# Seven quarter products for the second matmul too, in the last two token tiles

## The chip, the cores and the metric

The kernel runs on one core of one Trainium2 chip, in one launch. The metric is the device time of one execution in microseconds, the median of several runs. Lower is better.

## The reference

Linear attention per head, an RMS norm over the head's 64 outputs, and a feed-forward block over all tokens:

```python
kv = np.einsum('bhsd,bhse->bhde', k, v)                # 8 batches, 8 heads, 576 tokens, 64 wide
out = np.einsum('bhsd,bhde->bhse', q, kv)
rms = np.sqrt(np.mean(out * out, axis=-1, keepdims=True) + 1e-06)
x = out / rms * g_norm                                 # then laid out as 4608 tokens x 512
h = x @ w_in                                           # 512 x 2048
g = h * (1.0 / (1.0 + np.exp(-h)))
return (g @ w_out).astype(np.float32)                  # 2048 x 512
```

Everything is float32 in and out.

## The kernel before

**Numbers as two parts.** Each operand of a matmul is held as an upper part (fp32r, by a ScalarE copy) and a lower part (the rest, by a subtraction), and a product is three matmuls: upper times lower, lower times upper, upper times upper. A matmul here is 128 x 128 weights against 128 x 256 moving columns. TensorE's weight loads are PEld in the profile.

**Tiles.** The 4608 tokens are nine tiles t = 0 to 8 of 512 (`TN`). The inner width of 2048 is 16 blocks `f` of 128 (`NF`), `w_in` in blocks `wi`, `w_out` in blocks `wo`. For a tile, the first product makes h of one block (128 x 512), the gate is SiLU on ScalarE, and the second product (`project`) adds the block's share to four banks of sums `acc`, one for 128 tokens each. PSUM has eight banks of 512 columns: two for h (`hp`), four `acc`, two `at` for the attention.

**Steps.** Tiles 0 and 1 go block by block. From tile 2 on `pair_step(t, i)` takes the blocks i and i + 8 together, i = 0 to 7; it counts as two steps g = 16 t + 2 i and g + 1. In it the first product is done by Winograd's form of Strassen's scheme: the 512 inputs, the 512 tokens and the pair of blocks are cut in halves, so four quarters of x and four of the weights, and seven products P1 to P7 of 6 matmuls each (`product`, 42 matmuls) take the place of eight (48). Sums of weight quarters were stored to DRAM in tile 1 (`make_sums`) and are loaded again for each step (`load_sums`); sums of the quarters of x (`sums_of_x`) and the seven operands' two parts (`make_operand`) are made in the last step of the tile before, ScalarE the upper, VectorE the lower parts. P1, P2 go to one `hp` bank, P6, P7 to the other, then P4, P5, P3; VectorE adds them up. Then comes the second product of the pair before, whose gated values have had a whole step: `due` and `project`, 2 blocks x 4 chunks of tokens x 6 = 48 matmuls.

**Order.** All is written out by hand; each engine runs its own list in order, and waits come from the data. Jobs of the next batch's attention stand at numbered steps in three lists, `first_jobs`, `mid_jobs` and `last_jobs` (`at`, `spread_out`): among them the x stage (`Pair.spread` and `Pair.scale`, L326 and L334), which turns attention output into the next tile's x. In tile 7 four of them remain, one for 128 input rows each, at g = 113, 114, 115 and 116. All transfers are issued by SyncE (SP). At the end of a tile the four banks are copied to `ob` by VectorE and ScalarE in turn and stored. In the last tile the last bank is split in two halves.

Of the kernel before, what the change touches and what calls it, by code (L numbers as in the profile page):

```python
# [8 lines left out]
F32 = mybir.dt.float32  # L9
F32R = mybir.dt.float32r  # L10
# [25 lines left out]
def linear_attention_rms_silu_ffn(  # L36
# [29 lines left out]
    CUT = 256  # L66
    LAG = 2
    WARM = 2

    const = ctx.enter_context(tc.tile_pool(name="const", bufs=1))  # L70
    weights = ctx.enter_context(tc.tile_pool(name="weights", bufs=1))
# [472 lines left out]
    HF, H = NF // 2, TN // 2  # L544
    low, high = slice(0, H), slice(H, TN)
    sums_in_dram = dram.tile([HF, 2, P, 2, 2 * H], F32, name="sums_in_dram")
    operands, x_sums, once = {}, {}, {}

    def order(t):
# [5 lines left out]
    def make_sums(i):  # L555

        lower, upper = (tmp.tile([P, S], F32, name=name, tag="tmp")[:, :TN] for name in ("lower", "upper"))
        sums = spare(0, [P, 4, H], F32, "sums")

        def whole(to, f):  # L560
            w = parts["wi", f].bitcast(F32)
            nc.vector.tensor_tensor(out=to, in0=w[:, 0, :], in1=w[:, 1, :], op=ALU.add)

        def combine(j, x, y, op=ALU.subtract):
            nc.vector.tensor_tensor(out=sums[:, j], in0=x, in1=y, op=op)

        def split(half):
            two = sums[:, 2 * half:2 * half + 2].rearrange("p j n -> p (j n)")
            both_parts = spare(1 + half, [P, 2, 2 * H], F32R, "sum_parts")
            nc.scalar.copy(out=both_parts[:, 0], in_=two)  # L570
            nc.gpsimd.tensor_tensor(
                out=both_parts[:, 1], in0=two, in1=both_parts[:, 0].bitcast(F32), op=ALU.subtract
            )
            nc.sync.dma_start(out=sums_in_dram[i, half], in_=both_parts.bitcast(F32))

        return [
            lambda: whole(lower, i),
            lambda: whole(upper, i + HF),
            lambda: combine(2, upper[:, low], upper[:, high], ALU.add),
            lambda: combine(0, sums[:, 2], lower[:, low]),  # L580
            lambda: combine(1, lower[:, low], upper[:, low]),
            lambda: combine(3, lower[:, high], sums[:, 0]),
            lambda: split(0),
            lambda: split(1),
        ]

    def move_a22(f):
# [59 lines left out]
        3: (3, lambda: quarter(1, high), of_sum(3)),  # L647
    }

    def make_operand(m):  # L650
        j, x, _ = seven[m]
        upper, lower = operand(j)[:, 0], operand(j)[:, 1]
        nc.scalar.copy(out=upper, in_=x())
        nc.vector.tensor_tensor(out=lower, in0=x(), in1=upper.bitcast(F32), op=ALU.subtract)

    def product(m, i, out):
        j, _, a_of = seven[m]
        x = operand(j)
        n = 0
        for c in range(2):  # L660
            for a, b in ((0, 1), (1, 0), (0, 0)):
                nc.tensor.matmul(  # L662
                    out=out, lhsT=a_of(i, a, c), rhs=x[:, b, c], start=(n == 0), stop=(n == 5)
                )
                n += 1

# [81 lines left out]
        return [(t, i + HF, hi[0], lo[0]), (t, i, hi[1], lo[1])]  # L748


    first_jobs, mid_jobs, last_jobs, chains = {}, {}, {}, {}

    def at(jobs, step, *calls):
# [5 lines left out]
    def spread_out(make, third, *counts):  # L759

        calls = []
        for n, count in enumerate(counts):
            def some(n=n, count=count):
                if not n:
                    calls.extend(make())
                for _ in range(count):
                    calls.pop(0)()
            at((first_jobs, mid_jobs, last_jobs)[(third + n) % 3], (third + n) // 3, some)

    def plan(b, g):  # L770
# [52 lines left out]
        def x_stages(p, s, segment):  # L823
            at(mid_jobs, s, lambda: p.spread(norms[1][:, p.c], segment), lambda: p.scale(segment))
            if segments(b)[segment][2] < 2:
                at(mid_jobs, s, lambda: p.to_tile(segment))

        for p in ps:
            if b == 1:
                n = SECOND[p.c][4]  # L830
                at_third(n, lambda p=p: p.spread(norms[1][:, p.c], 0), lambda p=p: p.scale(0))
                at_third(n, lambda p=p: p.to_tile(0))
            else:
                x_stages(p, s + 2 + p.c, 0)
            x_stages(p, b * NF + 1 + p.c, 1)
        return ps

    with tc.manual_schedule():
# [64 lines left out]
        def x(p, count, fast=False):  # L903
            part(xs, p, lambda: p.to_tile(fast), count)
# [91 lines left out]
        at(mid_jobs, NF + 14, lambda: make_operand(6))  # L996
        for t in range(2, NT):
            spread_out(sums_of_x, 3 * (t * NF - 3), 1, 1, 1, 1)

        pend, prepped = [], []  # L1000
        for t in range(NT):
            sums = sums_of(t)
            if t == 1:
                at_tags.append("other")
            if t >= 2:
# [37 lines left out]
            if t == 1:  # L1043
                for m in (7, 4, 5, 3):
                    make_operand(m)
        lower_part(*late_part.pop())
        for old in sums:
            for item, _ in pend:
                project(*item, *old)


_INS = ["q", "k", "v", "g_norm", "moe_w_in", "moe_w_out"]
# [38 lines left out]
```

## Time and profile before

| | |
|---|---|
| three runs, us | 817.03, 817.92, 817.62; median 817.62 |
| profiled execution, first to last instruction | 815.8 us, 1.8 less than that median |
| TensorE busy | 806.5 us, 99% of the span, 7484 matmuls |
| VectorE, ScalarE, GpSimd busy | 533.9, 361.6, 145.7 us |
| DMA | 122.82 MB, mean 151 GB/s |
| granted TensorE clock | 1.000 |

The profile knows the profiled execution's time as its span only; the runs' time has 1.8 us more around it. Busy times overlap: the engines work side by side, and a matmul counts as busy for 0.28 us though the next one starts 0.11 us after it. The chain of waits is followed back from the last instruction; the timeline has one row for one or several equal instructions with start and duration in microseconds, and in brackets what it had idled for.

### The profile page before, as it was taken

Reading aid. Unit: us, or ns where it says so; the run is one execution under the profiler, and the core shown is the slowest. Engines: PE = TensorE matmul, PEld = TensorE weight load, DVE = VectorE, ACT = ScalarE, POOL = GpSimd, SP = SyncE. Lnnn points to the kernel's source line nnn. Section 1 sums busy time; section 2 is a strip of 40 time slices with the busy share of each in tenths; the row PEclk is TensorE's granted clock in tenths of the full one; section 3 lists DMA queues with packets and bytes.
Section 4 is the critical chain, followed back from the end, with each engine's and each line's share of the span. In section 5 each row is a group of like instructions: output and inputs, shape, how many; then the busy total and the mean of one; then the engine's idle time right before and its main releaser. Section 6 shows DMA issues by size and latency. Waiting matters only on the chain.

```text
span 815.8 us, 18127 instructions
## 1 busy us (share of the span) xinstructions
PE 806.5 (99%) x7484; PEld 801.5 (98%) x7484; DVE 533.9 (65%) x1036; ACT 361.6 (44%) x753; POOL 145.7 (18%) x141
## 2 busy tenths in 40 slices
PE   7999999999999999999999999999999999999998
PEld 7899999999999999999999999999999999999998
DVE  4999956787566677656875767656865663464332
ACT  4887555434552355325532444245532432243222
POOL 2799783322110011000200020001100000000000
DMA  9994012356524444263436451445433343334321
GB/s 345 412 409 126 1 60 90 124 195 228 184 82 162 162 162 156 82 221 118 170 104 211 142 182 64 166 159 174 135 104 104 104 155 105 104 104 155 104 105 53
DMA packets 42277, 122.82 MB, mean 151 GB/s; under 512 B 4690, under 2 KB 4946, under 8 KB 42194
## 3 DMA queue, kind: packets, MB, share of 16 engines
q1 hardware_dynamic: 42194, 121.65, 42.4%
q8 instruction: 59, 0.97, 0.5%
q14 instruction: 24, 0.20, 0.1%
HBM read 103.81 MB, written 17.83 MB: 149 GB/s over the span
## 4 chain that ended last, share of the span: by engine, by line
PE 93%; DMA 4%; POOL 2%; issue 1%; SPq 1%; ACT 0%; POOLq 0%
PE acc L493 46%; PE hp L662 33%; PE hp L493 9%; DMA wo<-in_moe_w_out 3%; PE at L273 2%; PE at L306 1%; PE at L307 1%; PE at L308 1%; DMA early_wo<-in_q 1%; PE at L493 1%; POOL wo L212 1%; SPq L262 1%; POOL wi L212 0%; POOL gl L514 0%; POOL wo_full L178 0%
## 5 line engine op out<-in xcount | busy, mean ns | idle before, releaser
L493 PE MATMUL acc<-wo,gh 128*128 128x256 f32 x2272 | 354.6, 276 | 0.3 <-POOL wo L212 0.3
L493 PEld LDWEIGHTS acc<-wo,gh 128*128 128x128 f32 x2272 | 302.5, 188 | 0.7 <-POOL wo L212 0.5
L493 PE MATMUL acc<-wo,gl 128*128 128x256 f32 x1136 | 222.5, 276 | 0.0
L493 PEld LDWEIGHTS acc<-wo,gl 128*128 128x128 f32 x1136 | 171.7, 188 | 0.0
L662 PE MATMUL hp<-x_second,wi 128*128 128x256 f32 x1344 | 163.1, 276 | 0.0
L662 PEld LDWEIGHTS hp<-x_second,wi 128*128 128x128 f32 x1344 | 157.2, 188 | 0.0
L662 PE MATMUL hp<-operand,wi 128*128 128x256 f32 x1008 | 123.3, 276 | 0.0
L662 PEld LDWEIGHTS hp<-operand,wi 128*128 128x128 f32 x1008 | 118.4, 188 | 0.0
L294 POOL TENSOR_TENSOR ql<-q,qh 128x576 fp32r<-128x576 f32 x24 | 34.8, 1450 | 368.6 <-ACT qh L293 322.8
L713 ACT COPY wi<-hp 128x256 f32<-128x256 f32 x56 | 20.8, 372 | 136.5 <-PE hp L662 136.5
L671 ACT ACTIVATE gh<-gf 128x512 fp32r<-128x512 f32 x56 | 35.4, 632 | 91.9 <-DVE gf L726 80.4
L671 ACT ACTIVATE gh<-wi 128x512 fp32r<-128x512 f32 x56 | 35.5, 634 | 77.4 <-DVE wi L726 65.0
L714 DVE TENSOR_TENSOR gf<-hp,wi 128x256 f32<-128x256 f32 x28 | 11.9, 424 | 81.5 <-ACT wi L713 81.5
L714 DVE TENSOR_TENSOR wi<-hp,wi 128x256 f32<-128x256 f32 x28 | 11.9, 424 | 79.7 <-ACT wi L713 79.7
L493 PE MATMUL hp<-x_second,wi 128*128 128x256 f32 x384 | 46.3, 276 | 0.0
L675 DVE TENSOR_TENSOR gl<-wi,gh 128x512 fp32r<-128x512 f32 x56 | 38.4, 686 | 11.1 <-ACT wi L672 11.1
L493 PE MATMUL hp<-x,wi 128*128 128x256 f32 x360 | 44.5, 278 | 0.8 <-POOL x L444 0.8
L493 PEld LDWEIGHTS hp<-x_second,wi 128*128 128x128 f32 x384 | 44.9, 188 | 0.1
L675 DVE TENSOR_TENSOR gl<-gf,gh 128x512 fp32r<-128x512 f32 x56 | 39.3, 701 | 7.3 <-ACT gf L672 7.3
L493 PEld LDWEIGHTS hp<-x,wi 128*128 128x128 f32 x360 | 42.4, 188 | 1.2 <-POOL x L444 1.0
L715 DVE TENSOR_TENSOR wi<-hp,wi 128x256 f32<-128x256 f32 x56 | 23.8, 426 | 29.6 <-PE hp L662 29.6
L334 DVE SCALAR_TENSOR_TENSOR x<-o,gcol,yT 128x128 f32<-128x128 f32 (+7 forms) x52 | 41.2, 792 | 1.9
(143 smaller groups left out, 995.7 us busy)
## 6 DMA issues: line engine op xcount, KB each, us to landing
wi<-sums_in_dram SPq DMA_DIRECT2D x112, 512.0 KB, 3.4
out<-ob SPq DMA_DIRECT2D x35, 256.0 KB, 2.3
wi<-in_moe_w_in SPq DMA_DIRECT2D x16, 512.0 KB, 7.9
wo<-in_moe_w_out SPq DMA_DIRECT2D x16, 512.0 KB, 8.9
sums_in_dram<-sum_parts SPq DMA_DIRECT2D x16, 512.0 KB, 2.6
k<-in_k SPq DMA_DIRECT2D x28, 288.0 KB, 5.1
v<-in_v SPq DMA_DIRECT2D x28, 288.0 KB, 5.1
q<-in_q SPq DMA_DIRECT2D x28, 288.0 KB, 4.0
```

Of the source, the lines that this page charges most:

```text
L212: nc.gpsimd.tensor_tensor(out=w[:, 1, :], in0=full, in1=w[:, 0, :].bitcast(F32), op=ALU.subtract)
L262: nc.sync.dma_start(out=t, in_={"k": k, "v": v, "q": q}[name][self.b, self.c])
L273: nc.tensor.matmul(out=self.kv[h], lhsT=self.k[rows, c, :], rhs=self.v[rows, c, :], start=(start and r == 0), stop=(stop and r == 4),)
L294: (nc.vector if self.b == 1 else nc.gpsimd).tensor_tensor(out=self.ql, in0=self.q, in1=self.qh.bitcast(F32), op=ALU.subtract)
L334: nc.vector.scalar_tensor_tensor(out=to, in0=self.o[:, a:e], scalar=gcol, in1=self.yT, op0=ALU.mult, op1=ALU.mult)
L493: nc.tensor.matmul(out=to[:, at:at + 256], lhsT=stationary, rhs=moving[:, at:at + 256], start=start and at == 0, stop=stop and at == n - 256,)
L662: nc.tensor.matmul(out=out, lhsT=a_of(i, a, c), rhs=x[:, b, c], start=(n == 0), stop=(n == 5))
L671: nc.scalar.activation(out=gh, in_=x, func=AF.Silu)
L675: nc.vector.tensor_tensor(out=gl, in0=x, in1=gh.bitcast(F32), op=ALU.subtract)
L713: nc.scalar.copy(out=p1, in_=u)
L714: nc.vector.tensor_tensor(out=c1[:, low], in0=v, in1=p1, op=ALU.add)
L715: nc.vector.tensor_tensor(out=u2, in0=y, in1=p1, op=ALU.add)
```

## The change

From tile `OUT7` = 7 on, `seven_step(t, i, groups)` takes the place of `pair_step`, and `seven_end` ends the kernel. A tile's 512 tokens are two `Half` objects of 256. For each half and each pair of blocks j, j + 8, the second product too is cut in quarters (two chunks of 128 tokens, two blocks; two blocks, two halves of 256 output columns) and done by seven products of three matmuls, 42 for both halves where there were 48. Each of the seven sums of a half fills half a bank, 14 half banks in seven banks; they are added to over all eight pairs, and turned into the tile's output once per tile (`Half.results`: one ScalarE copy, seven VectorE additions of 256 columns, two stores, per half). The eighth bank is left for the first product, whose seven products follow each other there in four rounds: P1 and P6, P2 and P7, P4 and P5, P3. Between the rounds stand the second product's windows W0 to W3, of 12, 9, 12 and 9 matmuls, of the pair before (for tile 7's first step: 12 each, of tile 6's last pair, by `project`).

The second product's operands are quarters of the gated values and four sums of them, made per half and step (`first_forms`, `last_form`, then upper and lower parts). Sums of `w_out` quarters are made in tiles 3 to 6 (`make_out_sums`, on GpSimd, with two ScalarE copies, two VectorE subtractions and two stores to DRAM each) and loaded for each step (`load_out_sums`). The operands of tile 8's first product have their lower parts on GpSimd and VectorE in turn, and the x stage in tile 7 moves to g = 113, 116, 119 and 122.

```diff
+    def make_out_sums(j):
...
+        def split(half, two):
+            nc.scalar.copy(out=both_parts[:, 0], in_=two)
+            nc.vector.tensor_tensor(out=both_parts[:, 1], in0=two, in1=both_parts[:, 0].bitcast(F32), op=ALU.subtract)
+            nc.sync.dma_start(out=out_sums[j, half], in_=both_parts.bitcast(F32))
...
-    def make_operand(m):
+    def make_operand(m, engine=nc.vector):
...
-        nc.vector.tensor_tensor(out=lower, in0=x(), in1=upper.bitcast(F32), op=ALU.subtract)
+        engine.tensor_tensor(out=lower, in0=x(), in1=upper.bitcast(F32), op=ALU.subtract)
...
+    class Half:
+        order = 1, 2, 3, 5, 7, 6, 4
...
+        def multiply(self, j, *ms):
+            for m in ms:
+                for n, (g, a) in enumerate(((self.hi, 1), (self.hi, 0), (self.lo, 0))):
+                    nc.tensor.matmul(
+                        out=self.out[m], lhsT=g[m], rhs=self.weight(m, j, a),
+                        start=j == 0 and n == 0 and m in self.opens, stop=j == HF - 1 and n == 2,
+                        skip_group_check=True,
+                    )
+
+        def results(self, t):
...
+            return [
+                lambda: nc.scalar.copy(out=p1, in_=out_of[1]),
+                lambda: add(second[:, low], out_of[2], p1),
+                lambda: add(u2, out_of[6], p1),
+                lambda: add(u4, u2, out_of[5], ALU.subtract),
+                lambda: add(first[:, low], out_of[3], u4),
+                lambda: add(u3, out_of[7], u2),
+                lambda: add(first[:, high], u3, out_of[5], ALU.subtract),
+                lambda: store(first, 0),
+                lambda: add(second[:, high], out_of[4], u3),
+                lambda: store(second, 1),
+            ]
...
+    def seven_step(t, i, groups):
...
+        def window(n):
+            if groups:
+                old(2)
+            elif before:
+                which = (first, second)[n // 2]
+                which.multiply(j, *(which.order[:4], which.order[4:])[n % 2])
...
+        def prepare(*ms):
+            for n, m in enumerate(ms if fresh else ()):
+                make_operand(m, (nc.gpsimd, nc.vector)[n % 2])
...
+        product(1, i, u, True, False)
+        product(6, i, v, False, False)
+        if before:
+            first.upper_summed()
+            second.upper_plain()
+            second.first_forms()
+            second.last_form()
+            first.lower_summed()
+        nc.scalar.copy(out=p1, in_=u)
+        nc.vector.tensor_tensor(out=u2, in0=v, in1=p1, op=ALU.add)
...
+        prepare(1, 6)
+        window(0)
+        if before:
+            second.lower_plain()
+            second.upper_summed()
+            second.lower_summed()
+        run(mid_jobs.pop(g, ()))
+        product(2, i, u, False, False)
+        product(7, i, v, False, False)
+        nc.scalar.copy(out=first.gated[:, low], in_=u)
+        nc.vector.tensor_tensor(out=u3, in0=v, in1=p1, op=ALU.add)
...
+        prepare(2, 7)
+        window(1)
+        if ends:
+            run(first.results(t - 1))
...
+        product(4, i, u, True, False)
+        product(5, i, v, False, False)
+        nc.vector.tensor_tensor(out=first.gated[:, high], in0=u, in1=u3, op=ALU.add)
+        nc.vector.tensor_tensor(out=second.gated[:, high], in0=v, in1=u3, op=ALU.add)
+        first.gate()
+        first.upper_plain()
+        first.first_forms()
+        prepare(4, 5)
+        window(2)
+        run(mid_jobs.pop(g + 1, ()))
+        product(3, i, v, False, False)
+        nc.vector.tensor_tensor(out=second.gated[:, low], in0=v, in1=u2, op=ALU.add)
+        second.gate()
+        first.last_form()
+        first.lower_plain()
...
+        prepare(3)
+        window(3)
+        if ends:
+            run(second.results(t - 1))
...
+    def seven_end(t):
...
+        first.multiply(HF - 1, *first.order)
+        run(first.results(t))
+        second.multiply(HF - 1, 1, 2, 6, 5, 3, 7, 4)
+        run(second.results(t))
...
-            x_stages(p, b * NF + 1 + p.c, 1)
+            x_stages(p, b * NF + 1 + p.c * (3 if b >= OUT7 else 1), 1)
```

Three places show what moves. First, TensorE in a step of tile 8. Before, the seven products of the first matmul in two banks, then the first rows of the second product:

```order
L662 MATMUL hp<-operand_2947,wi_511 128x256 x6
L662 MATMUL hp<-operand_2951,wi_511 128x256 x6
L662 MATMUL hp<-operand_2986,wi_2943 128x256 x6
L662 MATMUL hp<-x_second,wi_2943 128x256 x6
L662 MATMUL hp<-x_second,wi_1165 128x256 x6
L662 MATMUL hp<-x_second,wi_2945 128x256 x12
L493 MATMUL acc<-wo_1338,gh 128x256 x4
L493 MATMUL acc<-wo_1338,gl 128x256 x2
```

After, the first half of a step: P1 and P6, W0 (products 1, 2, 3 and 5 of the first half; `s` is a loaded sum of weights), P2 and P7:

```order
L692 MATMUL hp<-operand_2948,wi_870 128x256 x6
L692 MATMUL hp<-operand_2987,wi_2944 128x256 x6
L859 MATMUL at<-wo_1064,gh 128x256 x2
L859 MATMUL at<-wo_1064,gl 128x256
L859 MATMUL at<-wo_1785,gh 128x256 x2
L859 MATMUL at<-wo_1785,gl 128x256
L859 MATMUL at<-wo_1064,gh 128x256 x2
L859 MATMUL at<-wo_1064,gl 128x256
L859 MATMUL at<-s,gh 128x256 x2
L859 MATMUL at<-s,gl 128x256
L692 MATMUL hp<-operand_2952,wi_870 128x256 x6
L692 MATMUL hp<-x_second,wi_2944 128x256 x6
```

The second product's matmuls now stand in short windows between rounds that all use one `hp` bank, and each round waits for VectorE's last reading of that bank.

Second, VectorE where tile 7's output is read, at the start of tile 8. Before, the two output copies of VectorE stand between one step's last lower part and the next step's additions:

```order
L675 TENSOR_TENSOR gl<-gf,gh 128x512
L538 COPY ob<-acc 128x512 x2
L714 TENSOR_TENSOR gf<-hp,wi_3138 128x256
L715 TENSOR_TENSOR wi_3138<-hp,wi_3138 128x256
L716 TENSOR_TENSOR wi_3138<-hp,wi_3138 128x256
```

After, the first half's seven additions (L874) stand between the additions on P7 (L981) and on P4 and P5 (L992, L993):

```order
L981 TENSOR_TENSOR wi_3139<-hp,wi_3139 128x256
L874 TENSOR_TENSOR ob<-at,e_9914 128x256
L874 TENSOR_TENSOR e_9914<-hp,e_9914 128x256
L874 TENSOR_TENSOR e_9915<-e_9914,at 128x256
L874 TENSOR_TENSOR ob<-at,e_9915 128x256
L874 TENSOR_TENSOR e_9915<-hp,e_9914 128x256
L874 TENSOR_TENSOR ob<-e_9915,at 128x256
L874 TENSOR_TENSOR ob<-acc,e_9915 128x256
L992 TENSOR_TENSOR gated<-hp,wi_3139 128x256
L993 TENSOR_TENSOR gated<-hp,wi_3139 128x256
```

The second half's seven come in the same way after `first.lower_plain` (L815), ahead of the next forms (L822, L825, L830), the lower part `gl` (L836) and the addition on P6 (L968).

Third, VectorE at the very end. Before, two lower parts and two copies:

```order
L731 TENSOR_TENSOR gf<-hp,gf 128x256
L675 TENSOR_TENSOR gl<-wi_3138,gh 128x512
L675 TENSOR_TENSOR gl<-gf,gh 128x512
L538 COPY ob<-acc 128x512 x2
```

After, from P3's reader (L1001) to the first of the fourteen additions:

```order
L1001 TENSOR_TENSOR gated<-hp,wi_3139 128x256
L830 TENSOR_TENSOR wi_8882<-gated,wi_8882 128x128
L815 TENSOR_TENSOR gl<-gated,gh 128x384
L822 TENSOR_TENSOR wi_8882<-gated 128x256
L825 TENSOR_TENSOR wi_8882<-gated,wi_8882 128x128
L836 TENSOR_TENSOR gl<-wi_8882,gh 128x512
L830 TENSOR_TENSOR wi_8882<-gated,wi_8882 128x128
L815 TENSOR_TENSOR gl<-gated,gh 128x384
L836 TENSOR_TENSOR gs<-wi_8882,gs 128x512
L874 TENSOR_TENSOR ob<-at,e_10804 128x256
L874 TENSOR_TENSOR e_10804<-hp,e_10804 128x256
```

Both halves' last splits, and then all the additions of both halves, come after the last round of the first product.

More of the change, by code (lines that the diff above doesn't have):

```diff
@@ L662, in product @@
                 nc.tensor.matmul(
-                    out=out, lhsT=a_of(i, a, c), rhs=x[:, b, c], start=(n == 0), stop=(n == 5)
+                    out=out, lhsT=a_of(i, a, c), rhs=x[:, b, c], start=start and n == 0, stop=n == 5,
+                    skip_group_check=not check,
                 )
@@ new lines, in linear_attention_rms_silu_ffn, with ring, load_out_sums @@
+    rings = {}
+    def ring(j, m):
+        at = j % 2, m
+        if at not in rings:
+            pool, tag = (opool, "o") if at == (1, 7) else (kvq, "kvq")
+            rings[at] = pool.tile([P, S], F32R, name="s", tag=tag)[:, :TN].rearrange("p (a n) -> p a n", a=2)
+        return rings[at]
+    def load_out_sums(j, *ms):
+        for m in ms:
+            half, w = {3: (1, low), 5: (1, high), 6: (0, low), 7: (0, high)}[m]
+            to = parts["wo", j][:, :, high] if m == 3 else ring(j, m)
+            nc.sync.dma_start(out=to.bitcast(F32), in_=out_sums[j, half][:, :, w])
@@ L1045, in linear_attention_rms_silu_ffn @@
                     make_operand(m)
[L1046 to L1049, printed above, removed]
+        seven_end(NT - 1)
 _INS = ["q", "k", "v", "g_norm", "moe_w_in", "moe_w_out"]
```

149 lines of the change are left out of this document (147 added, 2 removed).

## The prediction

> **What bounds the kernel now.** I read the page's head and chain first, then the chain by time, then the last tiles by stretch, then the timeline of single steps.
>
> ```profile
> span 815.8 us, 18127 instructions
> PE 806.5 (99%) x7484; PEld 801.5 (98%) x7484; DVE 533.9 (65%) x1036; ACT 361.6 (44%) x753; POOL 145.7 (18%) x141
> PE 93%; DMA 4%; POOL 2%; issue 1%; SPq 1%; ACT 0%; POOLq 0%
> ...
> 725.59 4.76 PE hp L662 x42
> 730.35 5.44 PE acc L493 x48
> 735.79 4.76 PE hp L662 x42
> ...
> 684.79:694.99 10.20, 10.20 (x93) 10.20 (x92) 4.01 (x8) 2.90 (x5) 0.00 (x0) 1.00 0.32 104
> ```
>
> TensorE is 93% of the chain. The three rows from the chain by time are one pair step of tile 7: 42 products of the first matmul (4.76), then 48 of the second (5.44), 10.20 us for 90, so 0.1133 us a matmul. In such a step (last row; columns: PE, PEld, DVE, ACT, POOL busy) TensorE never stops, VectorE works 4.0 us, ScalarE 2.9, GpSimd nothing. So a matmul less is 0.1133 us less, as long as VectorE and ScalarE keep up; before, 48 matmuls in a row cover them.
>
> **The saving.** A pair step's second product falls from 48 to 2 x 7 x 3 = 42 matmuls. Sixteen steps: 96 x 0.1133 = 10.9 us less.
>
> **What hand-overs cost.** The change cuts a step (9.52 us) into P1+P6, W0, P2+P7, W1, P4+P5, W2, P3, W3, where W are windows of the second product with 12, 9, 12 and 9 matmuls (1.36 or 1.02 us). All P write one bank, and the order of waits shows every P waiting for the last reader of that bank on VectorE. Prices:
>
> ```profile
> 645.39 0.37 ACT L713 COPY wi<-hp 128x256 f32<-128x256 f32 x1 [1.49 <-PE hp L662]
> 645.79 0.42 DVE L714 TENSOR_TENSOR wi<-hp,wi 128x256 f32<-128x256 f32 x1 [1.49 <-ACT wi L713]
> 646.75 0.43 DVE L715 TENSOR_TENSOR wi<-hp,wi 128x256 f32<-128x256 f32 x1 [0.53 <-PE hp L662]
> 647.21 0.42 DVE L716 TENSOR_TENSOR wi<-hp,wi 128x256 f32<-128x256 f32 x1
> 647.55 0.68 DVE L675 TENSOR_TENSOR gl<-gf,gh 128x512 fp32r<-128x512 f32 x1
> 648.34 0.69 DVE L726 TENSOR_TENSOR gf<-hp,wi 128x512 f32<-128x512 f32 x1
> 648.95 0.41 DVE L730 TENSOR_TENSOR wi<-hp,wi 128x256 f32<-128x256 f32 x1
> ...
> 812.36 0.28 PE L493 MATMUL at<-wo,gl 128*128 128x256 f32 x1
> 812.67 0.37 ACT L538 COPY ob<-at 128x256 f32<-128x256 f32 x1 [0.31 <-PE at L493]
> ...
> 54.86 0.37 ACT L313 COPY o<-at 128x256 f32<-128x256 f32 x1
> 55.27 0.19 PEld L306 LDWEIGHTS at<-ql,kh 128*128 128x128 f32 x1 [0.93 <-ACT o L313]
> 55.28 0.41 PE L306 MATMUL at<-ql,kh 128*128 128x320 f32 x1 [0.74 <-ACT o L313]
> 55.52 0.31 PE L307 MATMUL at<-qh,kl 128*128 128x320 f32 x1
> 55.67 0.31 PE L308 MATMUL at<-qh,kh 128*128 128x320 f32 x1
> ```
>
> A matmul takes 0.28 but gives way after 0.11, and its reader starts 0.03 after its end, so 0.20 after the block's nominal end. ScalarE to VectorE costs 0.03. On VectorE a 256-wide operation starts 0.34 after the one before, 0.46 if it reads that one's result; a 512-wide one occupies 0.61. TensorE resumes late: the bank was free at 55.23, and L307, 0.15 behind L306 in a stream, started at 55.52, so L306 counts as started at 55.37: 0.14 after the release.
>
> W1 is short. From P7's nominal end: ScalarE's copy of u 0.20 to 0.57, VectorE's addition 0.60 to 1.03, P4 at 1.17, but W1 lasts 1.02. **Wait 0.15 in fifteen steps, (7,1) to (8,7): 2.2 us.** It is bounded by 0.04 each (no delay on resuming) and 0.20.
>
> [...]
>
> The other windows are long enough for an idle VectorE. P1 has 0.24 to spare, P2 0.18. But VectorE now works about 6.6 us of 9.52 in a plain step (5 adds and 2 forms of 256, 4 pieces of 128, 2 of 384 and 2 of 512), and everything placed into its queue ahead of a bank's reader arrives at TensorE. Durations for that:
>
> ```profile
> L671 ACT ACTIVATE gh<-wi 128x512 fp32r<-128x512 f32 x56 | 35.5, 634 | 77.4 <-DVE wi L726 65.0 <-PE acc L493 6.9 <-PE at L493 2.9
> L653 ACT CAST operand<-x 128x512 fp32r<-128x512 f32 x14 | 8.0, 623 | 0.8 <-POOL sum_parts L571 0.8
> L538 DVE COPY ob<-acc 128x512 f32<-128x512 f32 x18 | 12.1, 683 | 6.3 <-PE acc L493 6.3
> L326 DVE STREAM_TRANSPOSE yT<-y 128x512 f32<-128x512 f32 x4 | 2.8, 704 | 0.0
> L334 DVE SCALAR_TENSOR_TENSOR x<-o,gcol,yT 128x512 f32<-128x512 f32 x4 | 3.0, 752 | 0.1
> L571 POOL TENSOR_TENSOR sum_parts<-sums,sum_parts 128x512 fp32r<-128x512 f32 x16 | 21.5, 1348 | 38.1 <-ACT sum_parts L570 38.1
> L287 DVE TENSOR_TENSOR kl<-kvm,kh x28: 275/282/1421, 51.3 to 582.3; 128x128 fp32r<-128x128 f32 x28
> ...
> 120.32 1.43 POOL L294 TENSOR_TENSOR ql<-q,qh 128x576 fp32r<-128x576 f32 x1 [2.81 <-ACT qh L293]
> 120.47 1.42 DVE L287 TENSOR_TENSOR kl<-kvm,kh 128x128 fp32r<-128x128 f32 x1
> ```
>
> Times below count from P4's first matmul. In a plain step: P5's readers L992 and L993 start at 1.56 and 1.90, SiLU runs 2.01 to 2.64, the forms start at 2.67 and 3.13, P3 ends 3.40, its reader L1001 runs 3.60 to 4.02, P1 is due at 4.42.
>
> **Steps (7,2), (7,3), (7,5): 1.1 us.** The x stage (0.70 + 0.75, before hidden in idle VectorE time) lies before L1001 in (7,3): transpose from 3.34, scaling from 4.09, L1001 4.76 to 5.19, P1 at 5.33 instead of 4.42: 0.9. In the other two it lies before the addition that frees P4: 0.1 each.
>
> **Step (7,0): 1.65 us.** An output copy (0.68) and the x stage stand before L1001, which ends 5.77; P1 comes at 5.92 instead of 4.76 (W3 has 12 here): 1.16. The queue is then late for `gl` of the first half, which the fourth product of W0 in (7,1) needs, and for P2: 0.5 more.
>
> **Steps (7,6) to (8,0): 5.3 us.** The sums of x (4 x 0.61 to 0.72) and three of seven operands (0.61 each) share VectorE with the forms; the other four lower parts go to GpSimd, 1.3 us each. Without mutual hindrance I get 0.1 + 1.0 + 0.2 for the sums and 1.0 + 0.1 for the operands (operand 5's lower part, waiting for its ScalarE copy at 4.24, pushes L1001 to 5.29): 2.4. But the pair at 120.32 shows a 0.28 us operation with two inputs in SBUF lasting 1.42 beside a GpSimd one; the forms, `gl` and operand parts are of that kind. If each meets one GpSimd operation, `gl` of (7,6) comes 1.0 later, L1001 of (7,7) 1.0 later, and the forms after it 0.9: 5.3. I take this, since both engines' inputs become ready within 0.3 us of each other; 2.4 is the lower end.
>
> [...]
>
> **Steps (8,0) and (8,1): 3.45 us.** Tile 7's results are 2 x 7 additions in VectorE's queue. The first seven (0.34 or 0.46 apart) end at 2.58, so L993 ends at 3.26 and P3 starts 3.42 instead of 2.72: 0.7. The second seven run 5.68 to 8.50, ahead of the second half's forms and the first half's `gl`, which ends 10.1; W0's fourth product needs it at 7.73 and gets it at 10.25: 2.5, and P2 0.2.
>
> **The end: 4.7 us.**
>
> ```profile
> out<-ob SPq DMA_DIRECT2D x35, 256.0 KB, 2.3
> ...
> out<-ob SPq DMA_DIRECT2D x2, 128.0 KB, 1.9
> ```
>
> Before, TensorE's last block ends nominally at 812.53 and the span 3.2 later: one copy of 0.37 and a 128 KB store. After, waits for `gl` aside, it would end at 9.18 on the clock of (8,7). VectorE, still splitting until 7.6, begins the fourteen additions there; the fourth of the second half writes a buffer that the first half's store holds (issued 10.1, landing 2.3 later), so it starts at 12.4; three more end at 14.0, the last 256 KB store lands at 16.35, and 0.75 follow as before: 17.1, that is 7.9 after TensorE against 3.2.
>
> **Costed at nothing.** The output weights' sums in tiles 3 to 6 (per pair of blocks six GpSimd operations, about 5.6 us, two ScalarE copies, two VectorE subtractions, two 512 KB stores) lie where GpSimd works four times 1.4 us per tile and VectorE waits over a microsecond for ScalarE's copy (1.49 above). The part that the first two thirds of a step take is done before the next pair's copy; if it came a microsecond late, P4 would wait, at most 0.3 us in each of eight places. The sums' loads, three or four of 256 KB per step, have a whole step (9.5 us) on a DMA share of 0.32; the two loads of 512 KB keep about 6 us each. I allow 0 to 2 us for both.
>
> **Sum.** -10.9 + 2.2 + 1.65 + 1.1 + 5.3 + 3.45 + 4.7 = +7.5. On the profiled span, 815.8, that is 823.3; the three runs' median, 817.62, lies 1.8 above the span, and with this unchanged the time is 825.1.
>
> **The rivals.**
> - *GpSimd and VectorE pass each other* (5.3 becomes 2.4): 822.2. For it: 27 of 28 L287 took about 0.28.
> - *VectorE's queue never holds TensorE*: only the end is left of the costs and the time is 817.6 - 10.9 + 4.7 = 811.4, faster. It decides if the waits inside the tiles, 13.7 in my sum, fall below 6.2. For it: VectorE has 2.9 us of slack in a plain step, and TensorE's waits may overlap more than a hand count sees. Against it: the fourteen additions alone need 5.5 us at the measured pitch, nearly twice that slack.
> - *Waits about half as long*, the end as computed: 817.6 - 10.9 + 6.9 + 4.7 = 818.3: no change to speak of, or a little slower.
> - *The clock falls in the waits.* The longest wait is 2.5 us in (8,1). If TensorE ran at half speed for the 30 matmuls after each of the two longest waits, that is 2 x 30 x 0.1133 = 6.8 more: 832.
>
> ```profile
> 0.00:100.00 100.00, 93.85 (x891) 90.60 (x892) 85.13 (x149) 67.90 (x145) 72.67 (x87) 1.00 0.69 264
> ```
>
> Against the last: in the first 100 us TensorE idles 6 us and the granted clock stays 1.00. [...]
>
> **How the numbers follow.** Chances: the sum as it stands 0.47; GpSimd and VectorE passing each other 0.22; waits half as long 0.13; VectorE never holding TensorE 0.11; the clock falling 0.05; a transfer late 0.02. The forecast is 825. The range 818.5 to 829.5 reaches down to the half-long waits and up by a quarter of the tile waits and the tail (18.4 x 0.25 = 4.6); the likeliest case's own is 823 to 828. What a measurement can tell from no change is 0.2%, 1.6 us: faster 0.12, same 0.08 (part of the half-long waits), slower 0.80.
>
> **What would show it.** 7388 matmuls instead of 7484. TensorE idle about 13 to 14 us between tile 7's start and its last matmul, released by VectorE: L968, L981 (0.15 a step), L1001, and L836's `gl`, the longest wait in (8,1). In the last 8 us VectorE adds and TensorE is done. [...]

## The result and the profile after

| | before | after |
|---|---|---|
| runs, us | 817.03, 817.92, 817.62, 817.19 | 836.62, 837.10, 834.72, 839.69 |
| median, us | 817.4 | 836.86 |
| profiled execution, first to last instruction, us | 815.8 | 834.7 |

The ratio is 1.024, interval 1.0219 to 1.0261: 19.5 us slower, where 7.5 was forecast. The runs after lie 5 us apart, those before 0.9.

The head of the page after (span, busy time of each engine, chain by engine):

```profile
span 834.7 us, 18341 instructions
...
PE 809.9 (97%) x7388; PEld 800.1 (96%) x7388; DVE 586.6 (70%) x1184; ACT 385.4 (46%) x816; POOL 200.9 (24%) x193
...
PE 82%; DVE 7%; DMA 5%; ACT 2%; POOL 2%; issue 1%; SPq 1%; DVEq 0%; ACTq 0%; POOLq 0%
```

The 96 matmuls are gone (7388), and VectorE, absent from the chain before, holds 7% of it. In what follows (t,i) is pair step i of tile t.

**Where the 19 us came from.** I compared the start of every pair step in the two traces. A clean step is 84 x 0.1133 = 9.52 us; what a step has above that falls into gaps between matmuls (stops), stretches at half clock, and stretches in which matmuls follow each other a little more slowly (the pitch is the time from the start of one to the start of the next). The two profiled spans differ by 19.0 (834.75 against 815.77):

| part | us | predicted |
|---|---|---|
| 96 matmuls less | -10.9 | -10.9 |
| stops in tiles 3 to 6 | +5.8 | 0 (bound 2) |
| stops in tiles 7 and 8, up to the last P4 | +13.3 | +13.7 |
| half clock after two of them | +3.2 | 0 (a rival at 0.05) |
| a pitch of 118 ns in place of 113, in tiles 7 and 8 | +2.7 | no term |
| the end | +4.7 | +4.7 |
| start, ahead of tile 2 | +0.2 | 0 |

Tile 7 begins at 649.8 in place of 643.8, though its own steps are the first that the change rewrites. The timeline of tile 3's second step shows how (the brackets give idle time and what ended it):

```profile
308.85 0.59 ACT L539 COPY ob<-acc 128x512 f32<-128x512 f32 x1 [2.47 <-DMA out<-ob]
309.33 0.62 ACT L602 CAST wi<-s 128x512 fp32r<-128x512 f32 x1
...
309.85 0.38 ACT L744 COPY wi<-hp 128x256 f32<-128x256 f32 x1
309.98 0.69 DVE L603 TENSOR_TENSOR wi<-s,wi 128x512 fp32r<-128x512 f32 x1 [2.50 <-ACT wi L602]
310.59 0.42 DVE L745 TENSOR_TENSOR gf<-hp,wi 128x256 f32<-128x256 f32 x1
...
311.07 2.31 PE L692 MATMUL hp<-x_second,wi 128*128 128x256 f32 x18 [1.09 <-DVE gf L745]
```

ScalarE's last output copy of tile 2 waits 2.47 us for a store to land. Behind it in ScalarE's queue stand a copy of the new sums and then L744, which the addition L745 needs and P4 after that. The same happens in tiles 4, 5 and 6. What ended the idle time ahead of the output copies (us in total, times), in the kernel after (L539) and before (L538, the same line):

```profile
  DMA out<-ob: 10.2, 4
...
  PE acc L493: 18.2, 20
```

Before, no output copy waited for a store.

In tiles 7 and 8, the stop in (7,7), then busy times and granted clock (PEclk, the third number from the right) by stretch:

```profile
724.84 1.41 POOL L684 TENSOR_TENSOR operand<-x,operand 128x512 fp32r<-128x512 f32 x1 [122.90 <-DVE wi L825]
...
725.04 1.75 DVE L836 TENSOR_TENSOR gl<-wi,gh 128x512 fp32r<-128x512 f32 x1
...
726.85 0.38 PE L859 MATMUL at<-s,gl 128*128 128x256 f32 x1 [1.77 <-DVE gl L836]
...
724.53:727.95 3.42, 1.65 (x12) 1.30 (x12) 3.39 (x6) 1.27 (x3) 1.41 (x1) 1.00 0.83 276
727.95:731.36 3.41, 3.41 (x18) 3.41 (x18) 1.65 (x4) 1.41 (x3) 0.84 (x1) 0.50 0.24 66
734.77:738.18 3.41, 1.84 (x16) 1.67 (x16) 2.54 (x6) 1.67 (x4) 1.27 (x1) 1.00 0.56 198
751.84:755.25 3.41, 1.33 (x10) 1.05 (x9) 3.34 (x9) 0.62 (x1) 0.00 (x0) 1.00 0.65 200
755.25:758.67 3.42, 3.42 (x18) 3.42 (x18) 0.58 (x2) 0.37 (x1) 0.00 (x0) 0.50 0.87 241
```

`gl` takes 1.75 us beside the GpSimd operation. In the 3.42 us that end at 727.95 TensorE is idle 1.77, in those that end at 755.25 2.08, and each time the next 3.41 us run at clock 0.50. In the stretch that ends at 738.18, 1.57 idle, the clock stays.

The end (store of the first half, VectorE's fourth addition of the second half, the last addition):

```profile
827.61 4.21 SPq L878 DMA_DIRECT2D out<-ob  x4
...
829.77 0.42 DVE L874 TENSOR_TENSOR ob<-acc,e 128x256 f32<-128x256 f32 x1 [0.74 <-DMA out<-ob]
...
830.90 0.42 DVE L874 TENSOR_TENSOR ob<-acc,e 128x256 f32<-128x256 f32 x1
```

TensorE's last matmul starts at 828.31. Without the 1.7 us of waits behind the last P3 its stream would end at 826.8, and the span ends 8.0 later; before, the last matmul starts at 812.36, so the stream ends at 812.47 and the span 3.3 later. So the end costs 4.7 more.

### The profile page after: what moved, and what is told of

It is laid out like the page before. It is cut to its first block, busy times and chain, and to the rows that moved or that the text cites. A ratio compares the mean times of both kernels' runs of the same rounds, so it can differ in the third digit from the quotient of the medians.

```text
span 834.7 us, 18341 instructions
## 1 busy us (share of the span) xinstructions
PE 809.9 (97%) x7388; PEld 800.1 (96%) x7388; DVE 586.6 (70%) x1184; ACT 385.4 (46%) x816; POOL 200.9 (24%) x193
## 4 chain that ended last, share of the span: by engine, by line
PE 82%; DVE 7%; DMA 5%; ACT 2%; POOL 2%; issue 1%; SPq 1%; DVEq 0%; ACTq 0%; POOLq 0%
PE acc L494 32%; PE hp L692 29%; PE hp L494 9%; PE acc L859 4%; DMA wi<-in_moe_w_in 3%; PE at L859 2%; PE at L274 2%; PE hp L859 1%; DMA out<-ob 1%; DVE gl L706 1%; DMA k<-in_k 1%; PE at L307 1%; PE at L308 1%; PE at L309 1%; DVE x L335 1%
## 5 line engine op out<-in xcount | busy, mean ns | idle before, releaser
L494 PE MATMUL acc<-wo,gh 128*128 128x256 f32 x1792 | 279.5, 277 | 0.0
L494 PEld LDWEIGHTS acc<-wo,gh 128*128 128x128 f32 x1792 | 238.7, 188 | 0.4
L494 PE MATMUL acc<-wo,gl 128*128 128x256 f32 x896 | 174.5, 276 | 0.0
L494 PEld LDWEIGHTS acc<-wo,gl 128*128 128x128 f32 x896 | 135.0, 188 | 0.0
L596 POOL TENSOR_TENSOR s<-wo 128x512 f32<-128x512 f32 x16 | 23.8, 1500 | 156.9 <-DVE x L335 122.5
L744 ACT COPY wi<-hp 128x256 f32<-128x256 f32 x40 | 14.9, 372 | 89.0 <-PE hp L692 89.0
L702 ACT ACTIVATE gh<-gf 128x512 fp32r<-128x512 f32 x40 | 25.3, 633 | 56.5 <-DVE gf L757 52.2
L809 ACT ACTIVATE gated<-gated 128x512 f32<-128x512 f32 x32 | 20.3, 633 | 62.2 <-DVE gated L992 45.1
L702 ACT ACTIVATE gh<-wi 128x512 fp32r<-128x512 f32 x40 | 25.4, 635 | 38.7 <-DVE wi L757 34.7
L745 DVE TENSOR_TENSOR wi<-hp,wi 128x256 f32<-128x256 f32 x20 | 8.5, 424 | 46.2 <-ACT wi L744 46.2
L745 DVE TENSOR_TENSOR gf<-hp,wi 128x256 f32<-128x256 f32 x20 | 8.5, 423 | 40.5 <-ACT wi L744 40.5
L313 ACT ACTIVATE sq<-at 128x256 f32<-128x256 f32 (+1 forms) x56 | 22.9, 409 | 28.9 <-PE at L309 28.2
```

The source lines that it names most:

```text
L313: nc.scalar.activation(out=self.sq[:, self.w], in_=self.ps, func=AF.Square)
L494: nc.tensor.matmul(out=to[:, at:at + 256], lhsT=stationary, rhs=moving[:, at:at + 256], start=start and at == 0, stop=stop and at == n - 256,)
L596: nc.gpsimd.tensor_tensor(out=to, in0=w[:, 0, :], in1=w[:, 1, :], op=ALU.add)
L702: nc.scalar.activation(out=gh, in_=x, func=AF.Silu)
L744: nc.scalar.copy(out=p1, in_=u)
L745: nc.vector.tensor_tensor(out=c1[:, low], in0=v, in1=p1, op=ALU.add)
```

## The experiments

Each comes from the kernel after by the edit shown, if not said otherwise, and is set beside its 836.86; the kernel before ran along each time (816.8 to 817.6). In the diffs `...` marks what is left out, and comments are added. Each run has one profiled execution, and what its trace shows is set beside the profiled execution after, of 836.62.

### The output weights' sums two steps later

```diff
-            spread_out(lambda j=j: make_out_sums(j), 3 * (3 * NF + 8 * j), ...)
+            spread_out(lambda j=j: make_out_sums(j), 3 * (3 * NF + 8 * j + 2), ...)
```

> The only edit: the sums of the output weights in tiles 3 to 6 start two steps later (g = 50 + 8 j in place of 48 + 8 j). Theory: their two scratch tiles hold two of the five buffers of the pool that the output copies at a tile's start also use; the fourth copy then waits 2.5 us for a store, and ScalarE's copy of the first product behind it holds TensorE 1.36 to 1.52 us at the start of tiles 3 to 6, 5.8 in all. Moved, all four waits are gone: 836.9 - 5.8 = 831.1. Rival: the ScalarE copies and VectorE subtractions of the sums themselves stand ahead of the readers of the first product; moved, they do so at another place and in eight steps: 834 to 837.

**830.96 us** (ratio 1.0162, 1.0149 to 1.0176), 5.9 less, where 5.8 was expected. In tile 3's second step:

```profile
306.74 0.59 ACT L539 COPY ob<-acc 128x512 f32<-128x512 f32 x1 [0.57 <-PE acc L494]
...
308.10 0.37 ACT L744 COPY wi<-hp 128x256 f32<-128x256 f32 x1 [0.77 <-PE hp L692]
```

The copy waits for its bank alone, and the four stops are gone. In each of the four tiles a stop of 0.3 appeared in another step, where GpSimd's additions now stand beside VectorE's square roots; that these cause it was not tested. So the stops in these tiles fell by 4.6 in all, and that the time fell by 5.9 is in part luck: the profiled execution, 829.7, also has one half clock less (1.6; mean granted clock 0.995 in place of 0.993), since none follows the stop in (7,7) (see the growing stops below), and 1.4 less lost to the slower pitch.

### Windows of 11, 11, 11 and 9

```diff
-                which = (first, second)[n // 2]
-                which.multiply(j, *(which.order[:4], which.order[4:])[n % 2])
+                a, b = (0, 11, 22, 33, 42)[n:n + 2]
+                for which, at in ((first, 0), (second, 21)):
+                    if max(a, at) < min(b, at + 21):
+                        which.multiply(j, *which.order, part=slice(max(a, at) - at, min(b, at + 21) - at))
```

> The only edit: the 42 matmuls of the second product are cut into windows of 11, 11, 11 and 9 in place of 12, 9, 12 and 9. Theory: the wait at P4 (step time 9.71 against 84 x 0.1133 = 9.52, 0.19 in fifteen steps) is the shortness of W1 and goes: 836.9 - 2.9 = 834.0. If the pitch of 118 ns, in which TensorE runs for whole steps after some waits (2.7 us in all over 113 ns), is what a short stop leaves behind, most of that goes too: about 831.5. Rival: with W0 one matmul shorter P2 now waits as P4 did, and the time stays at 836 to 837.

**836.45 us** (1.0232, 1.0218 to 1.0246), not distinguishable from 836.86. Yet the stop at P4 is gone. Two steps of tile 8, in stretches:

```profile
762.94:772.83 9.89, 9.89 (x86) 9.89 (x85) 6.08 (x16) 3.96 (x9) 0.00 (x0) 1.00 0.55 187
772.83:782.73 9.90, 9.90 (x87) 9.90 (x85) 6.10 (x16) 3.97 (x9) 0.00 (x0) 1.00 0.55 185
```

TensorE is busy throughout, and the clock is 1.00, but 84 matmuls take 9.89 us, 117.8 ns each. After the kernel's last long stop, in (8,1), TensorE came out at that pitch and, stopping no more, kept it for all six steps that follow: 2.3 us lost. The profile has a second such stretch, 2.5 us, from the stop in tile 3 to the end of that tile. Against the trace after, the stops at P4 fell from 2.2 to 0.3, and one half clock is gone (1.6); the other stops grew by 1.2, of which 0.7 stand at P2, by 0.1 to 0.25 each, since W0 is shorter; and the slower pitch cost 2.5 more. So the wait was rightly explained, and its gain went into the pitch and into other stops. That the short stop at P4 brings the pitch with it is not borne out: without it the pitch stayed, and in the kernel after, where nearly every step has it, steps (8,2) to (8,6) take 9.71 or 9.86 to 9.88, and the pitch changes at that stop in both directions.

### The x stage at even steps

```diff
-            at(mid_jobs, s, lambda: p.spread(norms[1][:, p.c], segment), lambda: p.scale(segment))
+            at(mid_jobs, s, lambda: p.spread(norms[1][:, p.c], segment))
+            at(last_jobs if b >= OUT7 and segment else mid_jobs, s, lambda: p.scale(segment))
...
-            x_stages(p, b * NF + 1 + p.c * (3 if b >= OUT7 else 1), 1)
+            x_stages(p, b * NF + ((0, 4, 6, 8)[p.c] if b >= OUT7 else 1 + p.c), 1)
```

> The only edit: the four x stages of tile 7 stand at g = 112, 116, 118 and 120, the transpose after the second half's lower parts, the scaling after the addition on P7, in place of g = 113, 116, 119 and 122, where two of them stand ahead of P3's reader. Theory: the waits of 1.13 before (7,1), about 0.35 inside it and 0.87 before (7,4) go, VectorE being idle over a microsecond at both new places: 836.9 - 2.3 = 834.6. Rival: VectorE has no spare time there either and the additions that free P4 and P3 come late instead: 836 to 837.

**834.38 us** (1.0208, 1.0189 to 1.0228), 2.5 less, with runs from 832.6 to 836.5. The stops of 1.13 and 0.87 are gone. A new one of 1.2 stands in (7,2), with the DMA share (second number from the right) from 665 to 670:

```profile
674.27 0.98 PE L692 MATMUL hp<-operand,wi 128*128 128x256 f32 x6 [1.01 <-DMA wi<-sums_in_dram]
...
665.00:670.00 5.00, 5.00 (x41) 4.78 (x41) 2.15 (x6) 0.44 (x2) 0.00 (x0) 1.00 1.00 335
```

Step (7,1) comes 1 us sooner, and tile 6's four output stores, four loads of output sums and two loads of 512 KB now share the same microseconds. The DMA engines are full there, and P6's weights come late; in the trace after, the same stretch had a share of 0.88. That the full engines make them late is argued, not tested. The profiled execution is the slowest of the four, with 2.5 us of slower pitch in tile 3: it has about 1 less in stops and one half clock less than the profiled one after, and the same span.

### Tile 7's result additions spread

```diff
+        run(put_off[:6])      # second half, behind the addition on P6 of (8,1)
...
-            run(first.results(t - 1))
+        run(parts_of[:5])     # first half, behind the addition on P7; [5:6] behind first.gate()
...
-            run(second.results(t - 1))
+            run(parts_of[6:])
+            put_off.extend(second.results(t - 1))
```

> The only edit: the first half's seven result additions stand as 4, 1 and 2 in step (8,0), the second half's as 5 and 2 in step (8,1) behind the addition on P6, in place of seven in a row twice in (8,0). Theory: the waits of 0.53 at P3 of (8,0) and of 2.47 at W0 and P2 of (8,1) go, and with the long wait the half clock after it (1.6): 836.9 - 4.4 = 832.5. Rival: VectorE's load as a whole is what holds TensorE, and the additions hold P4 and W2 of (8,1) instead: 835 to 837.

**833.43 us** (1.0195, 1.0181 to 1.0209), 3.4 less. The stops of 0.53 and 2.47 and the half clock behind the latter are gone. So is the half clock of (7,7), though its stop stayed, and 2.5 us of slower pitch came in tile 5; both lie ahead of what the edit changes, which is (8,0) and (8,1) alone. Of the stops 0.3 came back at P2 and 1.2 in W1 of (8,1):

```profile
754.85 0.42 DVE L874 TENSOR_TENSOR ob<-acc,e 128x256 f32<-128x256 f32 x1
...
755.33 0.50 PE L859 MATMUL acc<-wo,gh 128*128 128x256 f32 x2 [0.90 <-DVE ob L874]
```

The last of the second half's additions reads product 4 from the bank that both halves share, and the first half's product 4 waits for it.

### All operands' lower parts on VectorE

```diff
-                make_operand(m, (nc.gpsimd, nc.vector)[n % 2])
+                make_operand(m)
```

> The only edit: the seven lower parts of tile 8's first-product operands are all made by VectorE, none by GpSimd. Theory: a GpSimd operation on SBUF blocks VectorE's operations with two SBUF inputs (lower part of the forms 1.75 us in place of 0.68, form 1.27 in place of 0.28, operand parts 1.34 in place of 0.68), so GpSimd costs more than the 0.61 each that it takes over. The waits of 2.15 in (7,7), 1.74 before (8,0) and 0.79 in it become about 1.0, 0.9 and 0.4, and the half clock after the first (1.5) goes: 836.9 - 3.9 = 833.0. Rival: GpSimd does take load off VectorE, and with seven parts of 0.61 in its queue in place of three the waits grow by 4 x 0.61: 839.

**835.60 us** (1.023, 1.0208 to 1.0252), 1.3 less, a third of what was expected; with runs from 833.9 to 838.6 the time alone does not tell it from the kernel after. `gl` in (7,7):

```profile
726.98 0.68 DVE L836 TENSOR_TENSOR gl<-wi,gh 128x512 fp32r<-128x512 f32 x1
...
727.72 0.38 PE L859 MATMUL at<-s,gl 128*128 128x256 f32 x1 [0.61 <-DVE gl L836]
```

Without a GpSimd operation beside it `gl` takes 0.68, and the stop shrinks from 2.15 to 1.0. The one before (8,0) goes from 1.74 to 1.1, those in (8,0) grow from 1.3 to 1.4. Steps (7,7) to (8,1) take 36.2 us where they took 40.9, both half clocks included. That is 4.7, more than expected, but 1.5 of it is the half clock of (8,1), whose stop stayed (2.5 before the edit, 2.6 with it) and here has none behind it (mean granted clock 0.997), and in this profile the stop in tile 3 was followed by 2.5 us of slower pitch, which the profile after does not have there. So the shorter `gl` and the shorter stops are shown in the trace, and their worth in the time is not.

### Stops put into the kernel before

```diff
-        nc.scalar.copy(out=p1, in_=u)
+        for _ in range(6 if i == 1 and 3 <= t < 7 else 1):
+            nc.scalar.copy(out=p1, in_=u)
```

> The kernel before, with one edit: in the second pair step of tiles 3 to 6 ScalarE copies the first product's u six times in place of once, so that the additions that free its bank come about 1.8 us later (5 x 0.36) and TensorE, which has 0.5 us to spare there, stops for about 1.3 us in four places. Theory: a stop can leave TensorE at a pitch of 118 ns, which lasts until the attention's small products at the end of the tile, about 2.5 us a tile, whatever made the stop. The time is then 817 + 5.2 = 822.2 in executions without it and 2.5 or 5 more in others, scattered over several us where the kernel before scatters over one. Rival: the slower pitch comes from something in the changed kernel (its transfers or its seventh bank), not from stops: 822.2 with all runs within 1 us and a pitch of 113 throughout.

**823.70 us** (1.0077, 1.0065 to 1.0089), runs from 822.63 to 825.25. Four stops of 1.4 us (the step 1.53 longer), and in the profiled execution a pitch of 113 after each: this run does not tell the theories apart. A variant with twelve stops (`4 + (t + i) % 3 if i in (1, 3, 5) and 3 <= t < 7`) does:

> The kernel before, with one edit: ScalarE copies the first product's u four to six times in the second, fourth and sixth pair step of tiles 3 to 6, so that TensorE stops there for about 0.7 to 1.6 us, twelve times. Theory: a stop alone can leave TensorE at a pitch of 118 ns; in the changed kernels 4 of 20 stops in these tiles did, so 2 or 3 of the 12 stops are followed by it, up to the next stop (20 us, 0.8 us lost each). Rival: it needs something of the changed kernel, and all 12 stops are followed by a pitch of 113. The time, about 817 + 12 x 1.1 = 830, hardly tells them apart; the profile does.

**836.76 us** (1.0238, 1.0221 to 1.0255), where about 830 was expected: the twelve stops cost 1.3 each in place of 1.1, and the slower pitch 2.6 in all. Rows of the first product, two after the stop at 402.96, and then those from the stop at 449.09 on:

```profile
411.79 2.20 PE L662 MATMUL hp<-operand,wi 128*128 128x256 f32 x18
...
414.85 2.20 PE L662 MATMUL hp<-x_second,wi 128*128 128x256 f32 x18
...
449.09 2.39 PE L662 MATMUL hp<-x_second,wi 128*128 128x256 f32 x18 [0.78 <-DVE gf L715]
456.96 2.28 PE L662 MATMUL hp<-operand,wi 128*128 128x256 f32 x18
459.08 2.99 PE L662 MATMUL hp<-x_second,wi 128*128 128x256 f32 x24
```

Eighteen matmuls show 2.20 or 2.28, so 4% more pitch, 113 against 118. Three of the twelve stops (at 449, 495 and 587) were followed by it, each up to the next stop or to the small attention products at the end of the tile. So nothing of the changed kernel is needed: stops made by extra copies alone are sometimes followed by it. What decides which ones was not found.

### Stops of growing length

The same edit with `2 * t` copies, so 6, 8, 10 and 12 in tiles 3 to 6.

> The kernel before, with one edit: in the second pair step of tiles 3, 4, 5 and 6 ScalarE copies the first product's u 6, 8, 10 and 12 times, so that TensorE stops for about 1.3, 2.0, 2.7 and 3.4 us. Theory: the granted clock falls to a half for 3.41 us where most of one of its windows of 3.41 us is idle: never at 1.3, by chance of the window's place at 2.0, always at 2.7 and 3.4, at up to 1.6 us each: 817 + 9.4 + 3 to 5 = 829 to 832. Rival: the clock falls only after a window that is idle as a whole (3.41 us), which none of these stops fills: 826.5, up to 831 by the slower pitch alone.

**833.95 us** (1.0228, 1.0184 to 1.0272; runs from 832.2 to 844.4, the profiled one 832.2), above the 829 to 832 expected; no trace shows the run of 844.4. The stops were 1.4, 2.2, 3.0 and 3.8. Stretches of one window each:

```profile
398.78:402.19 3.41, 1.67 (x14) 1.67 (x15) 2.12 (x5) 2.25 (x7) 0.93 (x1) 1.00 0.46 154
487.53:490.94 3.41, 0.87 (x8) 0.67 (x6) 0.16 (x1) 3.17 (x10) 0.00 (x0) 1.00 0.75 263
490.94:494.35 3.41, 3.09 (x14) 3.09 (x15) 3.34 (x7) 0.93 (x3) 1.86 (x1) 0.50 0.00 0
579.69:583.10 3.41, 0.89 (x8) 0.69 (x7) 0.00 (x0) 3.13 (x10) 0.00 (x0) 1.00 0.74 273
583.10:586.52 3.42, 2.27 (x10) 2.28 (x11) 2.68 (x6) 1.72 (x5) 1.54 (x1) 0.50 0.02 5
```

With 1.74 of 3.41 us idle the clock stayed; with 2.54, in a stop of 3.0, it fell. After the stop of 3.8 it stayed low for two windows, the second with 1.15 us idle. The rival, that a whole window must be idle, falls: no window was. In these rows the border lies near 1.8 of 3.41 us, and they do not place it closer: after 1.77 idle the clock fell in the kernel after, and after 1.76 and 1.80 it did not with even windows.

```profile
724.51:727.92 3.41, 1.65 (x15) 1.45 (x13) 3.33 (x6) 2.22 (x5) 1.40 (x1) 1.00 0.95 311
734.75:738.16 3.41, 1.61 (x15) 1.44 (x14) 2.68 (x5) 1.67 (x4) 1.27 (x1) 1.00 0.67 235
```

Within an execution all these stretches lie on one grid of 3.41 us (727.95 and 755.25 are eight windows apart). The stop of (7,7), 2.1 to 2.4 long, was followed by half clock after, and not with the sums later, with even windows, with the x stage at even steps or with the results spread (mean granted clock 0.993 after, and 0.995, 0.995, 0.995 and 0.997 in these); that its place in the grid decides is an estimate, not tested.

### Everything together, and the end

Beside the windows, the x stage, the spread results and VectorE's lower parts (but for one operand) as above:

```diff
-            spread_out(lambda j=j: make_out_sums(j), 3 * (3 * NF + 8 * j), ...)
+            spread_out(lambda j=j: make_out_sums(j), 3 * (3 * NF + 8 * j + (0 if j % 2 else 2)), ...)
...
+                spread_out(sums_of_x, 3 * (t * NF - 6) + 1, 1, 1, 0, 0, 0, 0, 1, 1)    # t > OUT7
...
+        if ends:
+            make_operand(4)
+            make_operand(5)      # behind the addition on P6 of (8,0)
...
+            make_operand(3, nc.gpsimd)      # behind the addition on P7 of (8,0)
...
+        load_out_sums(i, 5, 7, 6)      # now behind load_sums(i + 1, 0)
...
+                outs = ends[:, 0], ends[:, 1]      # the last half's output buffers
```

> All of it together: the even pairs' output-weight sums two steps later, windows of 11, 11, 11 and 9, the x stages at g = 112, 116, 118 and 120, the sums of x between g = 122 and 124, the sums' loads of the second product behind that of the first, operands 1, 6, 2, 7 by VectorE in (7,7), 4 and 5 by VectorE and 3 by GpSimd in (8,0), tile 7's result additions spread over (8,0) and (8,1) with the one that reads the shared bank early, and at the end the fourth sums first and two output buffers of their own. Theory: each cause has its own place, so the gains add: 836.9 - 5.8 (sums) - 2.9 (windows) - 2.3 (x stages) - 2.7 (results) - 3.9 (sums of x and operands) - 3.0 (half clock) - 1.2 (end) = 815.1, and with no stop left to come out of in the slower pitch another 2.7 less, 812.4. Rival: VectorE is simply full from (7,5) to (8,1), and what is moved holds TensorE elsewhere: 820 to 826.

**813.38 us** (0.995, 0.9936 to 0.9963): 0.5% faster than the kernel before, where 812.4 was expected. Stretches of the profile: (7,1) to (8,6), of these (7,7) to (8,1), and the last five:

```profile
654.16:788.32 134.16, 133.99 (x1178) 133.55 (x1177) 99.91 (x242) 60.26 (x123) 1.60 (x1) 1.00 0.66 223
711.69:740.72 29.03, 29.00 (x254) 28.75 (x253) 26.46 (x66) 16.09 (x34) 1.60 (x1) 1.00 0.67 226
740.72:788.32 47.60, 47.60 (x422) 47.60 (x421) 30.32 (x76) 19.85 (x41) 0.00 (x0) 1.00 0.60 206
```

Fourteen steps take 134.16, 0.9 above 14 x 9.52, and the last five 9.52 each: no stop, no half clock, pitch 113. The profiled execution is 811.26 and another run 811.10; the other three, 813.4 to 814.0, lie where one stretch of slower pitch would put them, but no trace shows one of them. The rival, a VectorE that is full, falls: it works 26.5 of 29.0 us in (7,7) to (8,1), and TensorE loses 0.5 there.

Then the end: four of the fourteen additions by a ScalarE copy and a GpSimd addition, the last stores in halves, and tile 6's output copies all on ScalarE.

```diff
+                def aside(n, to, m, y):
+                    nc.scalar.copy(out=sides[:, n], in_=out_of[m])
+                    nc.gpsimd.tensor_tensor(out=to, in0=sides[:, n], in1=y, op=ALU.add)
...
-            (nc.scalar.copy if n % 2 else nc.vector.tensor_copy)(out=ob, in_=bank)
+            (nc.scalar.copy if n % 2 or t == OUT7 - 1 else nc.vector.tensor_copy)(out=ob, in_=bank)
```

> As all_moved, with the output copies of tile 6 all on ScalarE, and at the very end ScalarE and GpSimd taking four of the fourteen result additions (a copy of the bank, then an addition in SBUF) and the last output stored in halves. Theory: the end is VectorE's queue of fourteen additions of 0.37 and the last store, so it gets shorter by 4 x 0.37 = 1.5 and by 0.4 for the smaller store; the stop of 0.4 in (7,1) goes with the two output copies ahead of VectorE's addition: 813.4 - 2.3 = 811.1. Rival: GpSimd's additions (0.74 each, after a copy of 0.37) end last in place of VectorE's, and the time stays at 813 to 814.

**810.08 us** (0.9919, 0.9907 to 0.9931). Four runs lie from 809.8 to 810.3 and two at 812.3 and 812.4, 2.5 apart, as much as one stretch of slower pitch. The median is 3.3 lower than that of the run above, but most of this is luck, since there the median fell into the upper group and here into the lower. The two profiled executions differ by 0.9 (811.26 and 810.34), and the expected gain was 2.3: the end, which was to give 1.9 of it, gave 0.9.

## Why the prediction was wrong

The forecast was 825.1 and the median is 836.86, 11.8 more. Three things that the sum put at nothing make up 11.7 of it in the profiled execution.

**The step that failed** is the paragraph "Costed at nothing". It counted the instructions of the output weights' sums, found idle time for them on GpSimd, VectorE and ScalarE, and bounded the harm by 0.3 us in each of eight places. It did not count their two scratch buffers, which come from the pool of five that the output copies use. Four copies waited for a store, 10.2 us in all, with ScalarE's next copies of the first product behind them, and TensorE stopped for 1.4 to 1.5 us in four places, 5.8 in all. With the sums made two steps later the copy no longer waits and the four stops are gone.

**The clock.** The rival existed, with a price of 6.8 and a chance of 0.05, and was set aside because the clock had stayed at 1.00 in the first 100 us of the trace before, with TensorE idle for 6. After two stops of 2.1 and 2.5 the clock fell to 0.50, at 1.6 each. The price was about twice too high: no run shows its 30 matmuls at half speed for each wait; the clock was low for 3.41 us, and the matmuls started 0.213 us apart there (six from 729.31 to 730.59), which is 16. In the window ahead of the first, 1.77 of 3.42 us idle, 52%, was enough.

**The pitch.** Each matmul was priced at 113 ns, since the trace before shows nothing else. That trace has no stop after 56 us. The slower pitch cost 2.7 us in the profiled execution, and may be behind much of the 5 us of scatter in the runs. What brings it on stays open.

**What held.** The saving, 10.9. The stops inside tiles 7 and 8, 13.3 against 13.7, and in their places: short W1 2.2 (2.2), (7,0) and (7,1) 1.7 (1.65), x stage 1.0 (1.1), sums of x and operands 5.1 (5.3), results 3.2 (3.45). W1's stop is 0.14 to 0.20 a step (0.15 in the sum; 0.26 in (7,2), beside the x stage), and two of the fifteen steps, behind the half clocks, have none; a stop of 0.04, the sum's lower bound (0.6 in all), is ruled out. The end, 4.7 (4.7), with the fourth addition waiting for the store as foretold; the sum's 812.53 for the end of TensorE's last block before should be 812.47, which makes its term 4.6. Choosing the value in which VectorE and GpSimd hinder each other was right: `gl` took 1.75 us beside a GpSimd operation in (7,7), against a median of 0.68. The rivals "pass each other", "half as long" and "never holds" fall by the same rows.

## What to carry to other kernels

When a stage is added in idle time, count its buffers too: list who else draws on the same pool at that time, and what stands behind a waiting copy in its engine's queue. Some stops of TensorE cost more than their length here: after two of 2.1 and 2.5 us the clock was 0.50 for 3.41 us, 1.6 lost each time, and after 3 of the 12 put into the kernel before the pitch was 118 ns in place of 113. So a scheme with fewer matmuls pays only when its hand-overs cost less than the matmuls it saves, 10.9 us here: the same arithmetic gave 836.9 with stops and 810.1 nearly without, about 2 of the difference being a shorter end.

## What the hardware showed that was not expected

- Two pitches at granted clock 1.00: 113 and 118 ns a matmul. The slower one was seen only after a stop (3 of 12 in the kernel before with stops put in), and with even windows it lasted for six steps of 9.89 us, 59 in all.
- The clock fell to 0.50 for 3.41 us after windows of 3.41 us with 1.77, 2.08 and 2.54 us idle; after windows with 1.74, 1.76 and 1.80 idle it stayed.
